# Attention and a soft mixture of experts on one core: undivided combine weights, row sums on TensorE, dispatched sums in q's PSUM bank

## The chip, the cores and the metric

The kernel runs on one core of one Trainium2 chip. The metric is the device time of one execution in microseconds (us), less is better. A run is named by the median of its executions.

## What is computed

Sliding-window causal attention over 8 batches, 8 heads, 576 positions and head size 64, and behind it a soft mixture of experts over the 4608 tokens that the attention gives (512 numbers each).

```python
scores = (1.0 / np.sqrt(D)) * np.matmul(q, k.transpose(0, 1, 3, 2))
rel = pos[:, None] - pos[None, :]
scores = np.where((rel >= 0) & (rel < 64), scores, -1000000000.0)
attn = softmax(scores, axis=-1)                    # with 1e-09 in the divisor
x = (attn @ v).transpose(0, 2, 1, 3).reshape(4608, 512)

logits = x @ phi                                   # phi: 512 x 32 slots
d = exp(logits - logits.max(0)); d /= d.sum(0)     # dispatch, over the tokens
slot_input = (d.T @ x).reshape(8, 4, 512)          # 8 experts, 4 slots each
slot_out[e] = np.maximum(slot_input[e] @ w1[e], 0) @ w2[e]   # hidden size 1024
c = exp(logits - logits.max(1)); c /= c.sum(1)     # combine, over the slots
out = c @ slot_out                                 # 4608 x 512, float32
```

## The kernel before

All inputs are float32 in memory and are cast to float16 by the loads themselves, which GpSimd issues into one queue (software_dynamic in the profile). The order of all work is written out by hand: the program order of each engine is the order of the calls, and an engine that waits holds everything behind it.

**The loop over pairs.** `n` counts 32 pairs of heads; four pairs make a batch. Step `n` works on several pairs at different stages: it transposes k of pair n+1 and q of pair n (L293), copies them to SBUF (L304, L309), takes the row maxima of pair n-1 from PSUM bank pair `a_m` (matmuls L319 and L322, VectorE's reduction L326, the ninth block in L332, L333 and L336), turns the maxima into a bias row (`st_shift`, L339 and L340), computes scores and their exponentials for pair n-2 (L345, L348, L354), multiplies pair n-4 with v (`st_av`, L378) and divides (L387, L388). `x_b` is the attention's output of a batch. v of odd rows is shifted by GpSimd (L166, L168) as soon as its load has landed, and PE's L378 needs the shifted copy. `loads(n)` issues the loads of q, k, v and of the expert weights, at fixed steps; a pool has four buffers for q and four for k, and the last expert's weights go through the same buffers (`load_last1` for w1 in four pieces `w1h`, `load_half` for w2 in two column halves of two loads each, `w2h`).

**The mixture's share of the loop.** Per batch `b`, spread over later steps: logits in columns 320 to 511 of bank `a_q` (L416), their running maximum, the exponentials `d` for the dispatch, their transposition, `fr_slots` (L503, L506: five matmuls that form the dispatched sums in `a_m`) and `fr_acc` (L514: VectorE adds them into `acc`), `fr_stat` (L446). Columns 448 to 511 of `a_q` hold -1e30, set once at L199, for the rows that have no token there. The combine weights: `fr_turn`, `cb_max` (L457), `cb_sub` on GpSimd (L462), `cb_exp` on ScalarE (L467), `cb_sum` on VectorE (L473, L474: sum over the slots and its reciprocal), `cb_mul` on GpSimd (L481), `cb_turn` (L486: transposition into `ct_all`).

**After the loop** the same steps follow in an order of their own for the last pairs, with `fill` matmuls (L624) in between, and then the experts: `first` (L793) multiplies the slots with w1 of four experts at a time, `turn_hidden` transposes, `second` (L814) multiplies with w2, for the left and the right half of the 512 columns (`ops[0]`, `ops[1]`, copied to `osb` at L879 and L883). `spread` (L646, L649) brings the combine weights of a batch into `ct4[k]`, two batches per `k`, through the tile `rp`, of which there is one. `give` (L872, L874, L876) forms the output: matmuls of 128 tokens with `osb` into one of four PSUM tiles `cp`, a copy of each tile to SBUF by ScalarE and VectorE in turn, and a store that SyncE issues. For k=0 the left half of the columns goes out first, in three stores, while the right half is still computed, then the right half in two; for k=1 to 3 nine stores of three rows of 512 columns each.

Of the kernel before, what the change touches and what calls it, by code (L numbers as in the profile page):

```python
# [18 lines left out]
def kernel(  # L19
# [178 lines left out]
    zero_q(0)  # L198
    nc.vector.memset(a_q[:, 448:512], -1.0e30)  # L199

# [229 lines left out]
    def fr_turn(b):  # L430
        lgT = pw.tile([128, 6, 32], FP32, name="lgT", tag="lgT") if b < B - 1 else lhf[0]
        nc.vector.transpose(lgT[:, :, :].rearrange("p i s -> p (i s)"), lgq[b][:, :])
        lgs[b] = lgT
# [11 lines left out]
    def fr_stat(b):  # L445
# [3 lines left out]

    lhf = [lh[:, 3 * i:3 * i + 3, :].rearrange("p i x -> p (i x)").bitcast(FP32).rearrange("p (i s) -> p i s", s=32)  # L450
           for i in range(2)]

# [12 lines left out]
    def cb_exp(b):  # L465
        ec = pw.tile([128, 6, 32], FP32, name="ec", tag="lgec") if b < B - 1 else lhf[1]
        nc.scalar.activation(ec[:, :, :], lgs.pop(b)[:, :, :], AF.Exp)  # L467
        cbs[b] = ec

    def cb_sum(b):  # L470
        pool = pw if b < B - 1 else pmo
        rs = pool.tile([128, 6], FP32, name="rs", tag="rs")
        nc.vector.reduce_sum(rs[:, :], cbs[b][:, :, :], axis=AXX)  # L473
        nc.vector.reciprocal(rs[:, :], rs[:, :])  # L474
        cbs[b] = cbs[b], rs

    def cb_mul(b, eng):
        ec, rs = cbs[b]
        cc = pw.tile([128, 6, 32], FP16, name="cc", tag="cc") if b < B - 1 else \
            lh[:, 6:8, :].rearrange("p i x -> p (i x)")[:, 0:192].rearrange("p (i s) -> p i s", s=32)  # L480
        eng.tensor_tensor(out=cc[:, :, :], in0=ec[:, :, :],  # L481
                          in1=rs[:, :].unsqueeze(2).broadcast_to([128, 6, 32]), op=ALU.mult)
        cbs[b] = cc
# [57 lines left out]
    for n in range(-1, NP - 1):  # L541
        loads(n)
        lb, eb, sb, cb = [of(n, lag) for lag in range(8, 12)]
        if of(n, 12) is not None:
            cb_sub(of(n, 12), nc.gpsimd)
        if of(n, 17) is not None:
            cb_mul(of(n, 17), nc.gpsimd)
        def maxima():
# [6 lines left out]

        if live(n - 3):
            st_score8(n - 3)
        early = n < 4
        if early and live(n - 1):
            maxima()  # L560
        if early and live(n):
            st_transpose(n, "qs", a_qh)
            st_copy_q(n)
# [43 lines left out]
        if sb is not None:  # L607
            fr_acc(sb, fr_slots(sb))
            fr_stat(sb)
# [6 lines left out]
        if of(n, 16) is not None:  # L616
            cb_sum(of(n, 16))
        if of(n, 19) is not None:
            cb_turn(of(n, 19))

# [20 lines left out]
    def spread(b, copy, rp=None):  # L641
        if rp is None:
            rp = psr.tile([128, 1024], FP32, name="rp", tag="rp")
        for t in range(5):
            w = 128 if t < 4 else 64
            nc.tensor.matmul(rp[:, 128 * t:128 * t + w], ss4[:, min(t, 3), :],  # L646
                             ct_all[:, b, 128 * (t // 4):128 * (t // 4) + w], start=True, stop=True,
                             skip_group_check=True)
        copy(out=ct4[b // 2][:, :, 64 * (b % 2):64 * (b % 2) + 64],  # L649
             in_=rp[:, 0:S].rearrange("p (x e) -> p e x", e=NE))  # L650

    b, p = B - 1, NP - 1
# [169 lines left out]
    cb_sub(b - 2, nc.gpsimd)  # L822
    cb_turn(b - 4)
    cb_sum(b - 3)
    cb_mul(b - 3, nc.gpsimd)
    first(0, 1)
# [8 lines left out]
    second(0, 0)  # L835
    cb_sum(b - 2)
    turn_hidden(1)
    spread(2, act)
    cb_mul(b - 2, nc.gpsimd)
    cb_turn(b - 3)  # L840
    cb_exp(b - 1)
    second(1, 0)
    spread(3, act)
    cb_sum(b - 1)
    cb_mul(b - 1, nc.gpsimd)
    cb_exp(b)
# [15 lines left out]
    def give(k, e0, ne, c0, nc_):  # L862
# [5 lines left out]
        for i0 in range(0, ne, n1):  # L868
            n_ = min(n1, ne - i0)
            cp = pst.tile([128, n1, nc_], FP32, name="cp", tag="cp")  # L870
            for i in range(n_):
                nc.tensor.matmul(cp[:, i, :], ct4[k][:, e0 + i0 + i, :], osb[:, c0:c0 + nc_],  # L872
                                 start=True, stop=True, skip_group_check=True)
            (act, dve)[turn % 2](out=ob[:, i0:i0 + n_, :], in_=cp[:, 0:n_, :])  # L874
            turn += 1
# [43 lines left out]
```

## Time and profile before

| | us |
|---|---|
| median of 3 runs (lowest, highest) | 194.87 (194.28, 195.09) |
| the profiled execution, its own time | 193.74 |
| its span in the trace | 192.0 |
| busy: TensorE, VectorE, ScalarE, GpSimd | 160.3, 140.1, 142.6, 102.2 |

The profiled execution's time is 1.74 us more than its span, for what lies around the program, and 1.13 us less than the median. In the rows of the profile PE is TensorE's matmuls, PEld its weight loads, DVE VectorE, ACT ScalarE, POOL GpSimd, SP SyncE. L12 is a line of the kernel. A row of the timeline has the start and the duration in us, then engine, line, operation, output and inputs by the program's names, shapes and a count; in square brackets stands how long the engine was idle just before, and what ended that. In a table by stretches the numbers behind a stretch are its length, the busy time of PE, PEld, DVE, ACT and POOL with the instructions in brackets, the share of its full clock that TensorE was granted (PEclk), the mean busy share of the 16 DMA engines, and what these moved in GB/s.

### The profile page before, as it was taken

To read this page: it belongs to the slowest core of one execution; us is meant where nothing else is said; L and a number is where in the kernel's file an instruction comes from. 1 tells how busy PE (TensorE), PEld (TensorE's weight loads), DVE (VectorE), ACT (ScalarE), POOL (GpSimd) and SP (SyncE) were. 2 spreads that over 40 slices of the span, in tenths; PEclk is the share of its full clock that TensorE was granted. 3 is DMA by queue.
4 is the path that set the end of the run, shared out by engine and by line. 5 is a ranking of instruction groups with operands and counts; after the bars stand their busy time and mean duration, and the time that the engine had idled before them with its cause. 6 is when DMAs were issued, how large, how long until landed. Compare 5 with 4: busy or idle time off the path is not lost.

```text
span 192.0 us, 6965 instructions
## 1 busy us (share of the span) xinstructions
PE 160.3 (84%) x2998; PEld 120.6 (63%) x2998; DVE 140.1 (73%) x347; ACT 142.6 (74%) x263; POOL 102.2 (53%) x131
## 2 busy tenths in 40 slices
PE   5696999989999998999999999989999899789000
PEld 1465878867777686777767786776785358542000
DVE  6683686887879779878978887897887746499100
ACT  5567979989799898989889888989578444588100
POOL 7968917455596555892993928665844133000000
PEclk9879999999999999999999999999999999999955
DMA  5999999999999999999999999999999999599995
GB/s 69 166 174 185 229 173 223 179 218 184 185 223 179 215 187 185 214 187 186 214 187 199 205 185 203 193 203 201 214 211 215 213 200 134 155 342 414 415 417 236
DMA packets 59774, 40.88 MB, mean 213 GB/s; under 512 B 38752, under 2 KB 55392, under 8 KB 58848
## 3 DMA queue, kind: packets, MB, share of 16 engines
q0 software_dynamic: 55536, 30.94, 115.6%
q1 hardware_dynamic: 4208, 9.50, 13.0%
q8 instruction: 23, 0.38, 0.7%
q14 instruction: 7, 0.06, 0.1%
HBM read 61.93 MB, written 9.44 MB: 372 GB/s over the span
## 4 chain that ended last, share of the span: by engine, by line
PE 47%; DVE 29%; ACT 7%; DMA 5%; issue 4%; POOL 0%; ACTq 0%; DVEq 0%; SPq 0%; POOLq 0%
DVE m L326 13%; PE a_m L319 6%; PE a_m L322 5%; PE a_v L378 5%; DVE x_b L388 4%; PE a_q L293 4%; DVE rt L340 3%; DMA out_dram<-w 3%; PE op L814 3%; PE a_k L293 3%; ACT qb L309 3%; DVE kT L301 2%; DMA qs<-in_q_dram 2%; PE a_s L345 2%; PE a_s L348 2%
## 5 line engine op out<-in xcount | busy, mean ns | idle before, releaser
L309 ACT ACTIVATE qb<-a_q 64x576 f16<-64x576 f16 x64 | 41.2, 644 | 7.0 <-PE a_q L293 6.2
L326 DVE TENSOR_REDUCE m<-a_m 128x8 f16<-128x1024 f32 x32 | 39.2, 1224 | 2.2 <-PE a_m L322 1.3
L354 ACT ACTIVATE pt<-a_s 128x1024 f16<-128x1024 f32 x32 | 32.8, 1024 | 6.5 <-PE a_s L348 5.1
L166 POOL COPY v<-v 64x1152 f16<-64x1152 f16 x16 | 18.2, 1140 | 28.1 <-DMA v<-in_v_dram 27.9
L388 DVE TENSOR_TENSOR x_b<-a_v,rc 128x640 f16<-128x640 f32 x31 | 25.5, 824 | 1.1
L322 PEld LDWEIGHTS <-qb 128*128 128x128 f16 x256 | 17.2, 99 | 8.5 <-ACT qb L309 1.4
L348 PEld LDWEIGHTS <-lh 128*128 128x128 f16 x288 | 18.8, 98 | 3.0 <-issue 2.6
L322 PE MATMUL a_m<-kT,qb 128*128 128x128 f16 x256 | 20.0, 222 | 0.1
L159 POOL DMA_DIRECT2D v<-in_v_dram x16 | 19.8, 1240 | 0.0
L406 ACT COPY xt<-a_k 128x576 f16<-128x576 f16 x28 | 17.9, 640 | 2.6 <-PE a_k L402 1.6
L319 PE MATMUL a_m<-wm,ident_h 128*128 128x512 f16 x64 | 19.7, 391 | 0.0
L345 PEld LDWEIGHTS <-kT 128*128 128x128 f16 x288 | 18.6, 98 | 1.6 <-issue 1.4
L345 PE MATMUL a_s<-qb,kT 128*128 128x128 f16 x256 | 19.5, 219 | 0.0
L348 PE MATMUL a_s<-rt,lh 128*128 128x128 f16 x256 | 19.5, 219 | 0.0
L168 POOL COPY v<-v 64x1088 f16<-64x1088 f16 (+1 forms) x16 | 17.9, 1117 | 0.8
L79 POOL DMA_DIRECT2D ks<-in_k_dram x17 | 11.7, 691 | 11.5 <-PE a_k L293 4.0
L340 DVE CAST rt<-a_v 9x128 f16<-9x128 f32 x30 | 8.7, 289 | 12.3 <-PE a_v L339 12.1
L378 PE MATMUL a_v<-v,pt 128*64 128x65 f16 x558 | 15.5, 196 | 2.3 <-DVE m L336 1.0
L304 ACT ACTIVATE kT<-a_k 128x576 f16<-128x576 f16 x25 | 16.3, 654 | 0.8 <-PE a_k L293 0.7
L293 PE MATMUL a_q<-ident_h,qs 96*64 96x96 f16 x384 | 15.4, 208 | 1.4 <-DMA qs<-in_q_dram 1.4
L378 PEld LDWEIGHTS <-pt 128*64 128x64 f16 x576 | 13.4, 110 | 4.5 <-DVE m L336 1.8
L293 PE MATMUL a_k<-ident_h,ks 96*64 96x96 f16 x384 | 14.6, 214 | 0.4 <-DMA ks<-in_k_dram 0.4
(174 smaller groups left out, 324.5 us busy)
## 6 DMA issues: line engine op xcount, KB each, us to landing
w<-in_moe_w_dram POOLq DMA_DIRECT2D x14, 1024.0 KB, 16.5
out_dram<-w SPq DMA_DIRECT2D x9, 768.0 KB, 8.8
qs<-in_q_dram POOLq DMA_DIRECT2D x16, 288.0 KB, 12.6
v<-in_v_dram POOLq DMA_DIRECT2D x16, 288.0 KB, 12.8
ks<-in_k_dram POOLq DMA_DIRECT2D x15, 288.0 KB, 15.4
out_dram<-w SPq DMA_DIRECT2D x2, 640.0 KB, 4.2
w1h<-in_moe_w_dram POOLq DMA_DIRECT2D x4, 256.0 KB, 16.1
w2h<-in_moe_w_dram POOLq DMA_DIRECT2D x4, 256.0 KB, 17.3
```

What stands on the lines that cost most here:

```text
L159: nc.gpsimd.dma_start(out=v1s[b % 2][:, c, 0:Dh], in_=v[b].rearrange("h s d -> (h s) d").rearrange("(c p) d -> p c d", p=128)[:, c, :])
L166: nc.gpsimd.tensor_copy(out=v2[64:128, c0:c1, 0:Dh], in_=v1[0:64, c0:c1, 0:Dh])
L293: nc.tensor.transpose(tq[64 * hf:64 * hf + 64, RP * r:RP * r + RP], src[0:RP, h + hf, Dh * r:Dh * r + Dh], ident_h[0:RP, 0:RP])
L309: nc.scalar.activation(qbs[p % NQ][h, :, hf, :], turned(a_qh)[h], AF.Copy, scale=QKS)
L319: nc.tensor.matmul(a_m[:, j, :], ident_h[:, :], wm[:, j:j + 4, :].rearrange("p c x -> p (c x)"), start=True, stop=False, skip_group_check= ...
L322: nc.tensor.matmul(a_m[:, i // 4, 128 * (i % 4):128 * (i % 4) + 128], qblock(p, i), kwindow(p, i), start=False, stop=True, skip_group_chec ...
L326: nc.vector.reduce_max(ms[p % 2][:, 64:72].rearrange("p (l c) -> p l c", l=2), a_m[:, :, :].rearrange("p l (c x) -> p l c x", x=128), axis ...
L345: nc.tensor.matmul(at(i), kwindow(p, i), qblock(p, i), start=(i % 4 == 0), stop=False, skip_group_check=True)
L348: nc.tensor.matmul(at(i), lh[:, i, :], rt[:, :], start=False, stop=True, skip_group_check=True)
L354: nc.scalar.activation(st_pt(p)[:, 0:8, :].rearrange("p i x -> p (i x)"), a_s[:, :, :], AF.Exp, scale=XS)
L378: nc.tensor.matmul(a_v[r0:r0 + 64, hf, 65 * (i // 2):65 * (i // 2) + 65], pt[:, i, 64 * hf:64 * hf + 64], rhs, start=True, stop=True, skip ...
L388: nc.vector.tensor_tensor(out=xbs[b][:, :, 128 * hp:128 * hp + 128].rearrange("p c (l d) -> p l c d", l=2), in0=avv[:, :, :, 0:64], in1=rc ...
```

## The change

Four things change. (1) In the loop `fr_slots` writes the dispatched sums into bank `a_q` in place of `a_m`; they cover all 512 columns, so VectorE sets columns 448 to 511 to -1e30 again behind `fr_acc`. (2) `cb_sum` and `cb_mul` go: `cb_exp` writes float16, and `cb_turn` transposes the undivided exponentials, three steps earlier. (3) A new function `sums(k)` multiplies the undivided weights in `ct4[k]` with a column of ones on TensorE, nine matmuls of one column into `rp`, and VectorE takes the reciprocals; the copies of the output multiply by them, one instruction per 128 tokens, since each has its own column of reciprocals. The stores for k=0, whose tiles held two groups of 256 columns, so take two copies per tile. (4) In the first four steps the ninth block's scores (`st_score8`) stand behind the maxima and not ahead of them.

```diff
-    nc.vector.memset(a_q[:, 448:512], -1.0e30)
+
+    def no_token():
+        nc.vector.memset(a_q[:, 448:512], -1.0e30)
+
+    no_token()
...
     def cb_exp(b):
-        ec = pw.tile([128, 6, 32], FP32, name="ec", tag="lgec") if b < B - 1 else lhf[1]
+        ec = pw.tile([128, 6, 32], FP16, name="ec", tag="ec") if b < B - 1 else \
+            lh[:, 6:8, :].rearrange("p i x -> p (i x)")[:, 0:192].rearrange("p (i s) -> p i s", s=32)
         nc.scalar.activation(ec[:, :, :], lgs.pop(b)[:, :, :], AF.Exp)
         cbs[b] = ec
-
-    def cb_sum(b):
...
-        nc.vector.reduce_sum(rs[:, :], cbs[b][:, :, :], axis=AXX)
-        nc.vector.reciprocal(rs[:, :], rs[:, :])
-    def cb_mul(b, eng):
...
-        eng.tensor_tensor(out=cc[:, :, :], in0=ec[:, :, :],
-                          in1=rs[:, :].unsqueeze(2).broadcast_to([128, 6, 32]), op=ALU.mult)
...
-        if of(n, 17) is not None:
-            cb_mul(of(n, 17), nc.gpsimd)
...
-        if live(n - 3):
+        early = n < 4
+        if live(n - 3) and not early:
             st_score8(n - 3)
-        early = n < 4
         if early and live(n - 1):
             maxima()
+        if live(n - 3) and early:
+            st_score8(n - 3)
...
         if sb is not None:
-            fr_acc(sb, fr_slots(sb))
+            fr_acc(sb, fr_slots(sb, a_q[:, :]))
+            no_token()
             fr_stat(sb)
...
         if of(n, 16) is not None:
-            cb_sum(of(n, 16))
-        if of(n, 19) is not None:
-            cb_turn(of(n, 19))
+            cb_turn(of(n, 16))
...
+    one = pmo.tile([128, 1], FP16, name="one")
+    nc.vector.memset(one, 0.0)
+    nc.vector.memset(one[0:32, :], 1.0)
+    rcs = pmo.tile([128, B // 2, NE], FP32, name="rcs")
+
+    def sums(k):
+        rp = psr.tile([128, 1024], FP32, name="rp", tag="rp")
+        for e in range(NE):
+            nc.tensor.matmul(rp[:, e:e + 1], ct4[k][:, e, :], one[:, :], start=True, stop=True, skip_group_check=True)
+        nc.vector.reciprocal(rcs[:, k, :], rp[:, 0:NE])
...
     first(1, 1)
     second(0, 0)
-    cb_sum(b - 2)
+    sums(0)
     turn_hidden(1)
     spread(2, act)
-    cb_mul(b - 2, nc.gpsimd)
-    cb_turn(b - 3)
     cb_exp(b - 1)
+    cb_turn(b - 2)
     second(1, 0)
     spread(3, act)
-    cb_sum(b - 1)
-    cb_mul(b - 1, nc.gpsimd)
     cb_exp(b)
-    cb_turn(b - 2)
+    cb_turn(b - 1)
+    cb_turn(b)
     for d in range(2):
         second(d, 1, range(3))
-    cb_sum(b)
-    cb_mul(b, nc.gpsimd)
-    cb_turn(b - 1)
-    cb_turn(b)
+    sums(1)
...
-            (act, dve)[turn % 2](out=ob[:, i0:i0 + n_, :], in_=cp[:, 0:n_, :])
+            for i in range(n_):
+                rc = rcs[:, k, e0 + i0 + i:e0 + i0 + i + 1]
+                if turn % 2:
+                    nc.vector.tensor_scalar(out=ob[:, i0 + i, :], in0=cp[:, i, :], scalar1=rc, scalar2=None, op0=ALU.mult)
+                else:
+                    nc.scalar.activation(ob[:, i0 + i, :], cp[:, i, :], AF.Copy, scale=rc)
             turn += 1
...
             give(k, e0, 3, 0, D)
-            if k < 3 and e0 < 6:
-                spread(2 * k + 2 + e0 // 3, (act, dve)[turn % 2])
+            if k < 3:
+                if e0 < 6:
+                    spread(2 * k + 2 + e0 // 3, (act, dve)[turn % 2])
+                else:
+                    sums(k + 1)
```

More of the change, by code (lines that the diff above doesn't have):

```diff
@@ L430, in fr_turn @@
     def fr_turn(b):
-        lgT = pw.tile([128, 6, 32], FP32, name="lgT", tag="lgT") if b < B - 1 else lhf[0]
+        lgT = pw.tile([128, 6, 32], FP32, name="lgT", tag="lgT") if b < B - 1 else lhf
         nc.vector.transpose(lgT[:, :, :].rearrange("p i s -> p (i s)"), lgq[b][:, :])
@@ L447, in fr_stat @@
                                 op0=ALU.mult, op1=ALU.add)
-    lhf = [lh[:, 3 * i:3 * i + 3, :].rearrange("p i x -> p (i x)").bitcast(FP32).rearrange("p (i s) -> p i s", s=32)
-           for i in range(2)]
+    lhf = lh[:, 0:3, :].rearrange("p i x -> p (i x)").bitcast(FP32).rearrange("p (i s) -> p i s", s=32)
     def cb_max(b):
@@ L822 @@
     cb_sub(b - 2, nc.gpsimd)
-    cb_turn(b - 4)
-    cb_sum(b - 3)
-    cb_mul(b - 3, nc.gpsimd)
+    cb_turn(b - 3)
     first(0, 1)
```

7 lines of the change are left out of this document (removed).

## The prediction

> **What bounds the kernel now.** I read the page first, its slices and its list of DMA issues, then the output phase by half microseconds.
>
> ```profile
> DMA  5999999999999999999999999999999999599995
> v<-in_v_dram POOLq DMA_DIRECT2D x16, 288.0 KB, 12.8
> 164.50:165.00 0.50, 0.46 (x5) 0.26 (x3) 0.45 (x1) 0.50 (x2) 0.00 (x0) 1.00 0.02 2
> 165.50:166.00 0.50, 0.50 (x7) 0.43 (x5) 0.34 (x1) 0.23 (x1) 0.00 (x0) 1.00 0.16 53
> 166.00:166.50 0.50, 0.27 (x3) 0.10 (x1) 0.00 (x0) 0.20 (x1) 0.00 (x0) 1.00 1.04 340
> 189.50:190.00 0.50, 0.00 (x0) 0.00 (x0) 0.00 (x0) 0.00 (x0) 0.00 (x0) 0.50 0.78 320
> ```
>
> The DMA engines are busy in every slice but the first, one near the end and the last. Half of the loads of v land 12.8 us or more after their issue, while the engines are busy: a load finds others queued ahead of it, and the queue does not run dry. The input is therefore one stream in the order of issue, whose landing times the engines' work does not move. One hole follows, around 164.5 (share 0.02). From 166.0 to 190 the output fills the DMA engines again. The end is thus: the last input lands, the experts' last matmuls and the first copies follow, the first store is issued, and about 24 us of stores follow.
>
> Next I asked each late load when it lands (start of its issue plus time to landing), and the timeline when it is used.
>
> ```profile
> L131 POOL DMA_DIRECT2D w1h<-in_moe_w_dram x2: 548/550/551, 137.3 to 137.9; - x2
> DMA to landing us min/median/max: 16.1/16.5/16.8
> L141 POOL DMA_DIRECT2D w2h<-in_moe_w_dram x1: 742/742/742, 145.1 to 145.1; - x1
> DMA to landing us min/median/max: 17.2/17.2/17.2
> L141 POOL DMA_DIRECT2D w2h<-in_moe_w_dram x1: 740/740/740, 147.6 to 147.6; - x1
> DMA to landing us min/median/max: 17.4/17.4/17.4
> 153.32 2.12 PE L793 MATMUL ha<-w,sit 128*32 128x512 f16 x35
> 155.72 0.38 PE L793 MATMUL ha<-w1h,sit 128*32 128x512 f16 x1
> 162.53 0.93 PE L814 MATMUL op<-w2h,hT 128*32 128x256 f16 x7
> 163.50 0.37 ACT L879 CAST qb<-op 128x256 f16<-128x256 f32 x1 [1.91 <-PE op L814]
> 164.38 1.35 ACT L874 COPY w<-cp 128x512 f32<-128x512 f32 x3 [0.51 <-PE cp L872]
> 164.99 15.94 SPq L876 DMA_DIRECT2D out_dram<-w  x14
> 165.22 1.05 PE L814 MATMUL op<-w2h,hT 128*32 128x256 f16 x8
> 166.30 0.37 ACT L883 CAST qb<-op 128x256 f16<-128x256 f32 x1 [0.57 <-PE op L814]
> ```
>
> The last two pieces of w1 land at about 153.5 and 154.7 (137.3 + 16.1, 137.9 + 16.8); the last is used at 155.72, 1.0 us later. The left half of w2 is complete at 145.1 + 17.2 = 162.3; its second load is used by the last four of the seven matmuls from 162.53, at 162.86, 0.6 us later. The right half is complete at 165.0 and its second load used by the fifth of the eight from 165.22, at about 165.7. So work ahead of the experts that ends earlier can bring the first store forward by at most 0.6 us.
>
> **The loop: the dispatched sums leave `a_m`.** One such step:
>
> ```profile
> 80.25 1.23 DVE L326 TENSOR_REDUCE m<-a_m 128x8 f16<-128x1024 f32 x1
> 81.53 0.40 PE L503 MATMUL a_m<-x_b,dT 128*32 128x512 f16 x4 [0.46 <-DVE m L326]
> 82.35 0.75 DVE L514 SCALAR_TENSOR_TENSOR acc<-acc,al,a_m 128x512 f32<-128x512 f32 x1 [0.68 <-PE a_m L506]
> 83.01 0.27 DVE L446 TENSOR_SCALAR stat<-stat,al,s 128x1 f32<-128x1 f32 x1
> 83.20 0.21 DVE L387 RECIPROCAL rc<-a_v 128x10 f32<-128x10 f32 x1
> L199 DVE MEMSET a_q<- 128x64 f32 x1 | 0.1, 112 | 0.1
> ```
>
> TensorE waits 0.46 for VectorE's maxima to leave `a_m`, then VectorE waits 0.68 for the sums. In `a_q`, which was copied out earlier in the step, the five matmuls run 0.5 earlier, beside the maxima, and VectorE's addition follows the maxima at once: 0.6 earlier, less 0.1 for the new memset of 0.11. The memset waits for the addition on VectorE itself; behind it stand L446 and the division, so its price is in the 0.1. TensorE's transpositions of the next q into `a_q` must now wait for the addition (and perhaps the memset), which end near 82.6; they stand behind the multiplication with v, which takes TensorE to about that time, so this wait costs 0 to 0.1 and holds only the next maxima. Gain 0.5 a batch, six times, the first at 48 us.
>
> **The loop: no sum, no division of the weights.** The transposition of `cb_turn` is only moved.
>
> ```profile
> L473 DVE TENSOR_REDUCE rs<-ec 128x6 f32<-128x192 f32 x7 | 2.4, 340 | 0.5 <-ACT ec L467 0.5
> L474 DVE RECIPROCAL rs<-rs 128x6 f32<-128x6 f32 x8 | 1.5, 192 | 0.3
> 15.04 0.22 PE L345 MATMUL a_k<-qb,kT 128*128 128x128 f16 x1 [0.82 <-ACT kT L304]
> 51.24 1.09 POOL L168 COPY v<-v 64x1088 f16<-64x1088 f16 x1
> 52.42 0.36 PEld L378 LDWEIGHTS <-pt 128*64 128x64 f16 x17 [0.31 <-DVE m L336]
> ```
>
> VectorE loses 0.53 a batch, four times inside the loop, at most 2.1; part of it lies under TensorE's multiplication with v, which the division awaits anyway, so I take 0.3 each, 1.2. GpSimd loses a multiplication a batch; it waits for landings in most steps, so nothing there. The scores moved behind the maxima in the first steps save at most the 0.82 at 15 us. But all that is saved before 52 us is lost again: the shifted v is ready at 51.24 + 1.09 = 52.33, just behind a landing, and used at 52.42. So 0.82 and the first 0.5 count nothing, and the loop saves 5 x 0.5 + 1.2 = 3.7, at most; I take 3.5, with 2 to 4 as bounds. The experts' first matmul comes at 149.8 in place of 153.32.
>
> **The stall that follows.** From 149.8 the first 40 matmuls of L793 take 2.2 us, four at a time, then TensorE stands from about 152.1 to 153.5 and again from 153.8 to 154.7 for the last two pieces of w1. Of the 3.5 us only 1.0 is left behind it, and that not by any engine but by the stream of loads.
>
> ```profile
> 5.00:7.00 2.00, 0.62 (x22) 0.43 (x16) 1.75 (x5) 0.65 (x1) 2.00 (x3) 1.00 1.26 180
> 8.00:12.00 4.00, 3.92 (x42) 2.38 (x41) 2.36 (x7) 2.63 (x5) 3.48 (x5) 0.57 1.62 150
> 12.00:14.00 2.00, 2.00 (x50) 1.83 (x48) 1.45 (x4) 1.37 (x3) 1.02 (x2) 1.00 1.44 188
> ```
>
> TensorE busy for 0.62 of two microseconds was followed by four in which it was granted 0.57 of its clock, though busy all the time. The stall, about 2.2 us idle of three, is as thin. Whether it lowers the clock is a rival below; the sum goes without. The Trainium skill, "TensorE: Matmul & The Clock Gate", Part 1, lets the clock fall only after an idle window of about 3.4 us, and warns of gaps longer than that: by this rule stalls of 1.4 and 0.9 us with matmuls between cost nothing, and the time stays at 195.2. The rows differ from it, since matmuls ran in that stretch too.
>
> **The experts and the first store.** `sums(0)` and `sums(1)` stand in TensorE's order ahead of the left half's last matmuls.
>
> ```profile
> 158.84 0.32 PEld L646 LDWEIGHTS <-v 128*128 128x128 f16 x5
> L874 ACT COPY w<-cp 128x256 f32<-128x256 f32 x1 | 0.4, 390 | 0.0
> L874 DVE COPY w<-cp 128x256 f32<-128x256 f32 x1 | 0.4, 414 | 0.0
> L799 ACT ACTIVATE hs<-ha,emask 128x512 f16<-128x512 f32 x2 | 1.4, 689 | 2.4 <-PE ha L793 2.4
> L809 ACT COPY hT<-th 128x512 f16<-128x512 f16 x2 | 1.2, 582 | 1.3 <-PE th L808 1.3
> ```
>
> Five weight loads of 128 columns start 0.056 apart (0.32 less one of 0.1, by four), so nine take 0.5, and the two calls 1.0; bounds 0.4 (one lies in waits that TensorE has there) and 1.5. `rp` has one buffer, so `spread(2)` also waits for the reciprocal of `sums(0)` (0.19 by L474), which the transpositions between them hide. With 1.0 earlier at the start and 1.0 more work, the left half is ready at 163.5 as before, and 162.3 is no limit any more.
>
> ScalarE's copy of 256 columns is 0.39, and a scale from a column adds 689 - 582 = 107 ns, so 0.5; two, overlapping a little, take 0.95 in place of about 0.6 for the one of 512. VectorE's two take about 0.9. The first store leaves 0.35 later, at 165.3 (bounds 0.2 and 0.6). The right half follows: its matmuls wait for the first `cp` tile, 0.35 later, and ScalarE's five small copies last to 164.38 + 2 x 0.95 + 0.45 = 166.7, so L883 is at 166.7. Is the output's queue then ever empty? Before, bytes moved 0.9 us after the first issue. Now 256 + 256 + 640 KB at 340 GB/s last from 166.2 to about 169.7; the fourth store needs L883 and about 2 us, 168.7, plus 0.9: just in time. Later stores hold 768 KB, 1.9 us of transfer, and need three copies, about 1.1 us on two engines; the 27 scaled copies, `sums(2)` and `sums(3)` lie under the stores.
>
> **The sum.** Own time 193.74; experts -1.0 + 1.0; first copies +0.35; stores the same length: 194.1. On the median, 194.87 + 0.35 = 195.2 us. Its own range, with the bounds above (experts -0.6 to +0.5, copies 0.2 to 0.6) is 194.5 to 196.0.
>
> **Rivals.** *Half clock behind the stall.* For: the rows from 5 to 14 us. Against: with a loop that saves under 3 us the first stall is under 1 us. The four microseconds at 0.57 lost 4 x 0.43 = 1.7 us of full clock; behind the stall the matmuls are all on the path, so the same costs 1.7 there. It decides from about 2 us of idleness in three. 195.2 + 1.7 = 196.9, slower. Chance 0.17.
>
> *The saving does not reach the experts.* If the wait of the q transpositions for `a_q` takes the place of the one removed, or another load is late, less than 0.3 us is left at 153: then `sums` and copies stand uncovered, +1.35, 196.2. For: v was 0.09 us ahead at 52 us. Against: the waits at 80 us are plain and nothing else ended last there. Chance 0.12.
>
> *The path was in the engines, not in the loads.* The median is 1.13 us above the profiled execution; if the others lose that in the loop, the saved 3.5 absorbs it (195.2 - 1.13 = 194.1), and if the loads moved up as well, the whole would show: 194.87 - 3.5 + 1.35 = 192.7. I take 193.3, between them. For: 142 us of busy ScalarE. Against: the unbroken DMA row. Chance 0.13.
>
> **Chances.** Forecast 0.58, rivals 0.17, 0.12 and 0.13. Half a per cent, 0.97 us, is about what a measurement of this kernel can tell from no change. The forecast lies within it, the first two rivals above, the third below: faster 0.13, same 0.58, slower 0.29. The range takes in the forecast's own, the two slower cases, and the third rival in part: 193.9 to 196.9.
>
> **What would show it.** Right: the shifts of v and the late loads land when they did, within 0.5 us; VectorE's idle 0.68 before L514 is gone; L793 starts near 150 and waits for `w1h`; the first store leaves within 0.5 us of 165.3. Wrong: the last `w2h` lands a microsecond or more earlier; PEclk below 1.00 between 154 and 166; DMA share under 0.9 between 167 and 189; L793 not before 152.5.

## The result, and the profile after

| | before | after |
|---|---|---|
| median, run side by side (lowest to highest) | 194.98 (194.28 to 197.51) | 192.48 (192.22 to 192.86) |
| the profiled execution, its own time | 193.74 | 192.86 |
| its span | 192.0 | 191.1 |
| busy: TensorE, VectorE, ScalarE, GpSimd | 160.3, 140.1, 142.6, 102.2 | 161.9, 139.2, 144.6, 97.9 |

The ratio is 0.9885 (95% interval 0.985 to 0.992): the change makes the kernel 2.5 us faster by the medians and 2.2 by the ratio, where 195.2 and a range from 193.9 were forecast. Ratios are of undisturbed executions alone, medians of all, so the two differ a little in places. The two profiled executions are only 0.9 us apart; the rest of the difference is between executions that left no profile, and that is the first thing to explain.

The page of after answers to the first rows of before:

```profile
DMA  4999999999999999999999999999999999499996
v<-in_v_dram POOLq DMA_DIRECT2D x16, 288.0 KB, 12.7
```

The DMA engines are as full as before, with the same hole before the stores. The late loads of after, by the issue of two pieces of w1 and of the last load of either half of w2:

```profile
L131 POOL DMA_DIRECT2D w1h<-in_moe_w_dram x2: 543/548/553, 136.6 to 137.1; - x2
DMA to landing us min/median/max: 16.6/17.0/17.3
...
L141 POOL DMA_DIRECT2D w2h<-in_moe_w_dram x1: 747/747/747, 144.9 to 144.9; - x1
DMA to landing us min/median/max: 17.2/17.2/17.2
...
L141 POOL DMA_DIRECT2D w2h<-in_moe_w_dram x1: 740/740/740, 147.3 to 147.3; - x1
DMA to landing us min/median/max: 17.4/17.4/17.4
```

The last w1h lands at 137.15 + 17.3 = 154.45, the left half of w2 at 162.06, the right at 164.7: 0.2 before the times of the kernel before. The timeline of the experts and the first store in after:

```profile
152.07 2.12 PE L793 MATMUL ha<-w,sit 128*32 128x512 f16 x35
154.49 0.38 PE L793 MATMUL ha<-w1h,sit 128*32 128x512 f16 x1
157.20 0.38 PE L649 MATMUL rp<-one,v 128*128 128x1 f16 x9
161.47 0.38 PE L649 MATMUL rp<-one,v 128*128 128x1 f16 x9
161.78 1.05 PE L814 MATMUL op<-w2h,hT 128*32 128x256 f16 x8
162.87 0.37 ACT L877 CAST qb<-op 128x256 f16<-128x256 f32 x1 [2.28 <-PE op L814]
164.62 1.47 SPq L874 DMA_DIRECT2D out_dram<-w  x3
```

L793 starts 1.25 earlier, not 3.5, so TensorE does not stand before w1h: its last piece is used at 154.49, 0.04 after it landed. The loop itself saved more. From the first maxima to the last it took 127.31 us in after and 130.16 before, 2.85 less; but in this execution the first q landed at 7.89 in place of 6.59, and the first maxima came 1.60 later (11.16, 9.56). The transposition of the first q, before and then after:

```profile
6.63 0.45 PE L293 MATMUL a_q<-ident_h,qs 96*64 96x96 f16 x12 [1.38 <-DMA qs<-in_q_dram]
```

```profile
7.94 0.45 PE L297 MATMUL a_q<-ident_h,qs 96*64 96x96 f16 x12 [2.62 <-DMA qs<-in_q_dram]
```

Behind the last w1h the sums cost 0.3 us each (nine matmuls at 161.47, the next work at 161.78), and the first store leaves 0.37 earlier than before. It is followed by 26.5 us to the end of the span, before by 27.0.

One batch's first step, in after, and the next maxima of both kernels:

```profile
80.44 1.22 DVE L330 TENSOR_REDUCE m<-a_m 128x8 f16<-128x1024 f32 x1
82.01 0.75 DVE L503 SCALAR_TENSOR_TENSOR acc<-acc,al,a_q 128x512 f32<-128x512 f32 x1
82.84 0.11 DVE L201 MEMSET a_q<- 128x64 f32 x1
83.01 0.45 PE L297 MATMUL a_q<-ident_h,qs 96*64 96x96 f16 x12 [0.20 <-DVE a_q L201]
84.96 1.23 DVE L330 TENSOR_REDUCE m<-a_m 128x8 f16<-128x1024 f32 x1
```

```profile
85.01 1.22 DVE L326 TENSOR_REDUCE m<-a_m 128x8 f16<-128x1024 f32 x1
89.33 1.22 DVE L326 TENSOR_REDUCE m<-a_m 128x8 f16<-128x1024 f32 x1
93.71 1.23 DVE L326 TENSOR_REDUCE m<-a_m 128x8 f16<-128x1024 f32 x1
```

VectorE's idle 0.68 before the addition is gone but for 0.14; yet the step is 84.96 - 80.44 = 4.52 long where it was 85.01 - 80.25 = 4.76: 0.24 less. Most of the other half of the expected 0.5 stands in the fourth row: TensorE waits 0.20 for the new memset before it may write q into the bank. The two steps behind it, without sum and division of the weights, are 4.20 and 4.21 long in after (84.96, 89.16, 93.37), before 4.32 and 4.38.

### The profile page after: what moved, and what is told of

Read it like the earlier page. It is cut to its first block, busy times and chain, and to the rows that moved or that the text cites. A ratio compares the mean times of both kernels' runs of the same rounds, so it can differ in the third digit from the quotient of the medians.

```text
span 191.1 us, 7035 instructions
## 1 busy us (share of the span) xinstructions
PE 161.9 (85%) x3034; PEld 121.7 (64%) x3034; DVE 139.2 (73%) x347; ACT 144.6 (76%) x267; POOL 97.9 (51%) x123
## 4 chain that ended last, share of the span: by engine, by line
PE 50%; DVE 24%; ACT 8%; DMA 6%; issue 4%; POOL 1%; ACTq 0%; DVEq 0%; POOLq 0%
DVE m L330 9%; PE a_m L323 6%; PE a_m L326 6%; PE a_q L297 5%; PE a_v L382 4%; PE a_s L349 4%; PE a_s L352 4%; DVE x_b L392 3%; DMA out_dram<-w 3%; PE op L814 3%; DMA ks<-in_k_dram 3%; DVE acc L503 3%; ACT qb L313 2%; DVE rt L344 2%; PE a_k L406 2%
## 5 line engine op out<-in xcount | busy, mean ns | idle before, releaser
L326 PEld LDWEIGHTS <-qb 128*128 128x128 f16 x256 | 17.3, 99 | 8.5 <-ACT qb L313 1.3
L297 PEld LDWEIGHTS <-qs 96*64 96x64 f16 x384 | 12.2, 111 | 5.6 <-DMA qs<-in_q_dram 2.8
## 6 DMA issues: line engine op xcount, KB each, us to landing
w2h<-in_moe_w_dram POOLq DMA_DIRECT2D x4, 256.0 KB, 17.3
```

The costliest lines, as they stand in the source:

```text
L297: nc.tensor.transpose(tq[64 * hf:64 * hf + 64, RP * r:RP * r + RP], src[0:RP, h + hf, Dh * r:Dh * r + Dh], ident_h[0:RP, 0:RP])
L326: nc.tensor.matmul(a_m[:, i // 4, 128 * (i % 4):128 * (i % 4) + 128], qblock(p, i), kwindow(p, i), start=False, stop=True, skip_group_chec ...
```

## The experiments

**Before once more, and the parts alone.** The kernel before, unchanged, beside three kernels that have one part each:

```diff
 # p1_slots
-            fr_acc(sb, fr_slots(sb))
+            fr_acc(sb, fr_slots(sb, a_q[:, :]))
+            no_token()
 # p4_order
-        if live(n - 3):
+        if live(n - 3) and not early:
             st_score8(n - 3)
         if early and live(n - 1):
             maxima()
+        if live(n - 3) and early:
+            st_score8(n - 3)
 # p23_undivided: the diff of the change without these two
```

> The kernel before, unchanged, for the spread of its executions and for another profile of it. Theory A (the start differs between executions): in the profile of before the first q landed at 6.59, in the profile after at 7.89, and the median of before lies 1.1 us over its profiled execution. By A this profile has its first q between 6.6 and 7.9, the experts' first matmul L793 later by the same difference (153.3 to 154.6), and its own time is higher by it (193.7 to 195.0); the timed runs spread over 194.3 to 195.1. Theory B (the difference lies elsewhere, in the stream of loads or in the stores): the own time does not follow the first landing; L793 stays at 153.3 within 0.3 whatever the first landing.

> Before, with the dispatched sums in q's bank and the memset behind the addition, and nothing else of the change. By the steps of the two traces: the step with the sums is 4.52 in place of 4.76 us from one maxima to the next, six times: 1.4 us earlier at L793. Theory A (in a usual execution of before no load stands close enough to take it back): faster by 1.4 us, about 193.5. Theory L (the loads set the end, as predicted): w1h lands near 154.5 and its last use is 1.0 before that, so at most 1.0 of it is left: 194.0 or more.

> Before, with only the scores moved behind the maxima in the first steps. Between the first maxima and the fourth the trace after took 11.45 us, before 12.30: 0.85 less. Theory A: it comes through to the end, 194.0 to 194.2. Theory L, as predicted: it is lost again where the shifted v of the fourth pair of loads is used at 52 us, and the time is that of before, within 0.2.

> Before, with undivided weights, sums on TensorE and scaled copies alone; the dispatched sums stay in a_m and the order of the first steps as before. By the steps: in two of a batch's four steps 0.13 and 0.18 us less, three or four times, 0.9 to 1.2 us; two sums of 0.31 us and 0.26 at the first copies are spent, 0.88. Theory A: between no change and 0.4 us faster, 194.5 to 194.9. Theory L: up to 1.0 saved at w1h and 0.88 spent, 194.8 to 195.0. As predicted in the sum (copies 0.35, sums 1.0, saving 1.2 of which 1.0 counts): 195.2. If the copies or sums cost more at the end than the trace after shows, it is slower than 195.2.

| | median | of before in the same runs | ratio (95%) |
|---|---|---|---|
| before again | 194.61 | 194.53 | 1.0015 (0.9988, 1.0042) |
| slots alone | 193.26 | 194.53 | 0.9940 (0.9910, 0.9970) |
| order alone | 194.29 | 194.53 | 0.9962 (0.9934, 0.9990) |
| undivided alone | 194.59 | 194.53 | 0.9992 (0.9962, 1.0021) |

The parts add up to the whole within their intervals: -0.6, -0.4 and -0.1% against -1.15%. The slots bring 1.2 to 1.3 us, near six steps at 0.24 (1.4). That is the time of theory A; by theory L, the prediction's, at most 1.0 could pass the wait for w1h. The undivided weights bring nothing by themselves, again within theory A: what the loop gains, the sums and copies spend. The order brings 0.2 by the medians and 0.7 by the ratio (0.2 to 1.3), so these runs do not tell whether most of its 0.85 comes through. Its profiled execution lost most of it. Its ninth maxima came 0.74 before those of before (41.61, 42.35), its thirteenth 0.18 (59.05, 59.23), for between them TensorE met the shifted v of 52 us:

```profile
52.31 0.41 PE L378 MATMUL a_v<-v,pt 128*64 128x65 f16 x15 [0.40 <-POOL v L168]
```

That the saving of the first steps is lost there is what the prediction said. It does not hold in every execution: in both profiles of after TensorE did not wait for v at this place.

The second profile of before (own time 196.19, 2.45 over the first) refutes both theories in their first form. Its first q landed at 6.25, earlier than in the first profile, and yet its start was slower, by 0.36 because the second k landed later (7.74, 7.38), and for the rest by TensorE's rate:

```profile
8.41 1.03 PE L319 MATMUL a_m<-wm,ident_h 128*128 128x512 f16 x2
9.24 1.06 PE L322 MATMUL a_m<-kT,qb 128*128 128x128 f16 x8
11.61 1.01 PE L319 MATMUL a_m<-wm,ident_h 128*128 128x512 f16 x2
12.54 1.03 PE L322 MATMUL a_m<-kT,qb 128*128 128x128 f16 x8
23.36 1.23 DVE L326 TENSOR_REDUCE m<-a_m 128x8 f16<-128x1024 f32 x1
...
165.33 0.60 PE L814 MATMUL op<-w2h,hT 128*32 128x256 f16 x4 [0.41 <-DMA w2h<-in_moe_w_dram]
```

In the first profile of before the timeline reads at these places:

```profile
7.81 0.61 PE L319 MATMUL a_m<-wm,ident_h 128*128 128x512 f16 x2
11.77 0.65 PE L322 MATMUL a_m<-kT,qb 128*128 128x128 f16 x8
21.86 1.22 DVE L326 TENSOR_REDUCE m<-a_m 128x8 f16<-128x1024 f32 x1
```

And the table by stretches from 60 to 80 us (the last two columns are the DMA share and GB/s), the first profile and then the second:

```profile
60.00:80.00 20.00, 18.74 (x404) 15.31 (x402) 16.48 (x41) 17.82 (x34) 11.87 (x15) 1.00 1.57 194
```

```profile
60.00:80.00 20.00, 18.39 (x393) 15.14 (x392) 16.97 (x41) 17.76 (x34) 10.54 (x13) 1.00 1.68 186
```

A pair of 512 columns takes 0.61 at full rate and 1.0 at half. In the second profile TensorE ran at half from 6.3 to 14.2, in the first from 8.5 to 11.9, and the fourth maxima came at 23.36 in place of 21.86: 1.5 us. Besides, its DMA engines, always busy, moved 186 GB/s where the first had 194 between 60 and 80 us, and the last w1h landed at 157.7 in place of 154.7; this time before, too, waited for w2h (0.41). The delay arose around the loads of v: ten of the sixteen landed 2.4 to 3.4 us after the load ahead of them, in the first profile none more than 2.1 (why is not known). So executions of one kernel differ in two things: how long TensorE's start is slow, and how fast the stream of loads runs.

**Are the loads the limit of after?** Theory L says that they are; theory E says that the engines set the end. Four kernels: after once more; the sums moved out of the path; less work in the loop, by leaving out the dispatched sums of the batches 1 to 5 (`a_lite`, whose output misses them); and the same with the four loads of w1h left out as well.

```diff
 # a_sums_late
     second(0, 0)
-    sums(0)
     turn_hidden(1)
...
-    sums(1)
...
     second(0, 1, (3,))
+    sums(0)
...
     second(1, 1, (3,))
+    sums(1)
 # a_lite
-            fr_acc(sb, fr_slots(sb, a_q[:, :]))
-            no_token()
+            if sb == 0:
+                fr_acc(sb, fr_slots(sb, a_q[:, :]))
+                no_token()
+            else:
+                dts.pop(sb), xbs.pop(sb)
 # a_lite_now1h: the same, and in load_last1
-        a = pin.tile([128, F], FP16, name="w1h", tag="qs")
-        nc.gpsimd.dma_start(out=a, in_=w1_dram(last)[:, len(w1_t[last]), :])
-        w1_t[last].append(a)
+        w1_t[last].append(w1_t[0][len(w1_t[last])])
```

> The kernel after, unchanged, for the size of the difference and for a second profile of it. From the parts alone (slots -1.3, order -0.2, undivided +0.1 in medians): about 1.4 us under before if they only add up in medians, 2.1 by the ratios of undisturbed runs. Theory E (the engines set the end in a usual execution): a second profile with a warmer start than the first (first maxima before 10.5 in place of 11.16) has L793 earlier by the same and is shorter by up to 1 us. Theory L (the stream of loads sets the end): L793 earlier, but the last use of w1h and w2h stays within 0.2 of their landing, and the time moves only with the landings.

> After, with both sums moved behind the last matmuls of each half, where TensorE waits some 0.45 us for ScalarE's copy of the experts' output. Theory E: two times 0.31 us leave the path to the first store, 0.6 us faster than after. Theory L: in the profile after the left half's second load of w2 landed at 162.06 and was used at 162.23, so at most 0.2 comes through; TensorE then waits for w2h ahead of the fifth matmul of the half, as in the second profile of before (0.57 us). If the reciprocals come too late for the first copies, the first store does not move at all or is later.

> After, leaving out the dispatched sums, their addition and the memset for the batches 1 to 5 in the loop (the output misses them). Five steps of 4.5 us become about 3.85: 3 us less of engine work ahead of the experts. Theory E: 3 us faster than after, about 189.5. Theory L, which is the mechanism of the prediction: L793 starts near 149, TensorE waits for w1h, whose last landing stays near 154.5, and the end is at most 0.5 earlier than that of after: 192.0 or more. If the stall behind w1h also halves the clock, as the first rival of the prediction has it, 193.5.

> The same, and the four loads of w1h left out as well (the last expert uses the first one's w1, so its output is another): 1 MB less in the stream ahead of w2h, at 210 GB/s 5 us. Theory L: with the loads 5 us earlier the engines' saving comes through: 189 to 190, 2.5 to 3 us below the kernel that leaves out the sums alone. Theory E: no difference between the two, both near 189.5.

| | median | of before in the same runs | ratio (95%) |
|---|---|---|---|
| after again | 192.18 | 194.26 | 0.9873 (0.9828, 0.9918) |
| sums late | 192.12 | 194.26 | 0.9866 (0.9822, 0.9911) |
| lite | 193.51 | 194.26 | 0.9949 (0.9906, 0.9991) |
| lite, no w1h | 189.82 | 194.26 | 0.9745 (0.9692, 0.9798) |

The last two show the mechanism: less work ahead of the experts made the kernel 1.3 us slower than after (193.5 was expected if the stall halves the clock), and the same kernel without four loads is 3.7 us faster than that. The timeline of the lite kernel:

```profile
151.31 0.40 PE L796 MATMUL ha<-w,sit 128*32 128x512 f16 x3
153.23 0.38 PE L796 MATMUL ha<-w1h,sit 128*32 128x512 f16 x1 [1.52 <-DMA w1h<-in_moe_w_dram]
154.46 0.58 PE L796 MATMUL ha<-w1h,sit 128*32 128x512 f16 x1 [0.83 <-DMA w1h<-in_moe_w_dram]
```

Its table by stretches, cut where the granted clock changes (the last three columns are the granted clock, the DMA share and GB/s):

```profile
150.69:154.10 3.41, 1.42 (x23) 0.44 (x16) 1.01 (x2) 0.31 (x1) 0.50 (x1) 1.00 1.09 215
154.10:157.51 3.41, 3.05 (x25) 1.38 (x28) 0.68 (x2) 1.43 (x3) 0.51 (x1) 0.50 1.21 201
```

It is the prediction's stall in the prediction's place, with its first rival behind it: 1.52 and 0.83 us idle, then 3.41 us with the clock at half. L793 started at 149.16, near the 149.8 of the prediction, and the last w1h still landed at 154.4. It was used at 154.46, as in after (154.49), and yet the first store left at 165.93 in place of 164.62: the 1.3 us arise behind the stall. The Trainium skill, "TensorE: Matmul & The Clock Gate", Part 1, lets the clock fall after an idle window of about 3.4 us and makes of it a rule against idle gaps of that length. Here it fell after two shorter waits with matmuls between them, so the measurement decides against that rule for gaps.

The second profile of after (own time 191.88) started faster and met the stall in its mild form:

```profile
150.93 2.12 PE L793 MATMUL ha<-w,sit 128*32 128x512 f16 x35
153.30 0.40 PE L793 MATMUL ha<-w,sit 128*32 128x512 f16 x3
153.60 0.38 PE L793 MATMUL ha<-w1h,sit 128*32 128x512 f16 x1
163.69 1.47 SPq L874 DMA_DIRECT2D out_dram<-w  x3
```

Its last two loads of w1:

```profile
L131 POOL DMA_DIRECT2D w1h<-in_moe_w_dram x2: 546/550/553, 136.1 to 136.6; - x2
DMA to landing us min/median/max: 16.3/16.6/16.9
```

The last group of four at 153.30 is held by its w1h, which landed at 153.56 and ran at 153.60. So this execution is 0.98 shorter than the first, about what its loads were earlier (0.9), though its engines were 1.14 ahead: theory L, as far as one execution tells.

Moving the sums brought nothing in the time, though in the profile the stretch from the last L793 to L877 is 5.56 us in place of 6.47 and 6.43: the fifth matmul of the left half then used its w2h 0.04 after the landing (161.67, 161.63). The same profile, with an early start, shows such a stall at another place, the shifted v of 52 us (its timeline, then its table by stretches, cut where the granted clock changes):

```profile
51.38 0.22 PE L382 MATMUL a_v<-v,pt 128*64 128x65 f16 x2 [1.33 <-POOL v L166]
52.53 0.42 PE L382 MATMUL a_v<-v,pt 128*64 128x65 f16 x15 [0.93 <-POOL v L168]
```

```profile
50.12:53.54 3.42, 1.24 (x46) 1.06 (x46) 0.80 (x4) 1.27 (x3) 3.30 (x3) 1.00 1.95 188
53.54:56.96 3.42, 3.42 (x31) 2.80 (x27) 1.62 (x3) 2.13 (x4) 3.33 (x6) 0.50 1.15 226
```

Again two waits, 1.33 and 0.93, and the clock at half behind them. The next maxima came 3.2 us later than elsewhere in the loop, and the execution still took only 192.28.

**A later start, and fewer loads, in both kernels.**

```diff
 # b_late, a_late
-            st_copy_q(n)
+            for _ in range(2 if n == 0 else 1):
+                st_copy_q(n)
 # a_now1h, b_now1h: load_last1 as in a_lite_now1h
```

> Before, with ScalarE's two copies of the first pair's q done twice: 1.3 us more ahead of the first maxima, on the engines alone; the loads are issued as before. Theory A (in before the engines set the end, and the loads stand 0.6 to 1.0 behind them): 1.3 us later less what the wait for v at 52 us takes back in an execution with an early start, so 0.8 to 1.3 slower than before. If the loads set the end of before as well: 0 to 0.4.

> After, with the same two copies done twice. Theory L (the loads set the end of after, with 0 to 0.3 to spare): the 1.3 us vanish in the wait for w1h in executions with an early start and count in part in those with a late one: 0.1 to 0.6 slower than after's 192.2. Theory E (the engines set it): 0.8 to 1.3 slower, as in before.

> After, without the four loads of w1h (the last expert uses the first one's w1). Theory L: the stream ends 5 us earlier and no longer holds the experts; the engines' own end shows, 0.3 to 1.0 below after, about 191.5; the executions then spread as those of before do. Theory E: no change from 192.2.

> Before, without the four loads of w1h. Its loads have 0.6 to 1.0 us to spare in three of four profiles and stood in the way in one (w1h at 157.69, own time 196.19). Theory A (the start makes the difference between its executions): no change of the median, within 0.2, and the long executions remain. Theory D (late loads make it): the median falls by 0.5 or more and the executions above 195.5 go.

| | median | of before in the same runs | ratio (95%) |
|---|---|---|---|
| before, late | 195.49 | 194.20 | 1.0074 (1.0046, 1.0102) |
| after, late | 193.08 | 194.20 | 0.9938 (0.9913, 0.9963) |
| after, no w1h | 191.81 | 194.20 | 0.9881 (0.9854, 0.9907) |
| before, no w1h | 193.66 | 194.20 | 0.9974 (0.9949, 0.9999) |

Before loses the whole 1.3. After loses 0.6 to 0.9 against its two medians (192.48, 192.18) and 1.0 to 1.3 by the ratios: more than theory L said, and by the ratios as much as theory E. Its profile has the fourth maxima at 23.75, the last w1h landed at 154.40 and used at 155.28: with this start the engines set the end. The copies are not the whole of that delay, for in this profile the granted clock was 0.50 from 9.2 to 16.0 us, twice as long as in the first profile of after. Without w1h after gains 0.4 in the median and nothing by the ratio; before gains 0.5, and its longest executions remain (196.2 and 197.3 among twelve), so that neither the start alone (theory A) nor late loads alone (theory D) make the difference between its executions. So in after the engines and the loads are within half a microsecond of each other, and the execution decides which comes last; in before the engines are mostly later, not always.

**A faster start, and the load order at the end.**

```diff
 # b_warm, a_warm
         if early and live(n):
+            if n == 0:
+                warm_up(4)
             st_transpose(n, "qs", a_qh)
 # a_split; a_split_late is this with the sums late
-    load_w(13)
     for d in range(2):
+        for h in range(2):
+            nc.gpsimd.dma_start(out=w2_t[NRES - 1, 0][:, 4 * h:4 * h + 4, DH * d:DH * d + DH],
+                                in_=w2_dram(NRES - 1)[:, h, :, DH * d:DH * d + DH])
         load_half(d)
 # a_left_first: a_split_late, and
-    for d in range(2):
-        second(d, 1, range(3))
+    second(0, 1, range(3))
...
+    second(1, 1, range(3))
     second(1, 1, (3,))
```

> Before, with four more warm-up matmuls (128x512, on zeros and ones) between the transpositions of the first k and of the first q, where TensorE waits for the first q. In the profiles the matmuls from 6 to 14 us ran at half rate for 3.3 us in the profile of before and for 7.7 us in its second one, and the fourth maxima came at 21.86 and 23.36. Theory A (this start is why the median of before lies above its profile): more executions start at full rate, fourth maxima near 21.5, the median falls by 0.5 to 1.0. Theory D (the rate of the loads, which landed up to 3 us later in the second profile): the median does not move by more than 0.2.

> After, with the same four matmuls. Theory L: an earlier start only lengthens the waits for v at 52 us and for w1h: no change from 192.2, within 0.2, or slower where such a wait halves TensorE's rate behind it. Theory E: 0.5 to 1.0 faster.

> After, with the second layer of the seventh expert loaded in halves by columns, its right half behind the left half of the last expert: the left half of the output then needs 0.5 MB less of the stream, 2.4 us at 210 GB/s, and the last load lands when it did. Theory L (the left half's w2h sets the first store): w2h's left half lands near 159.7 and the first store leaves 0.2 earlier at most, since the sums keep the engines at 162.2: 192.0. Theory E: the same, no change. It is the base for the next one.

> The same with both sums behind the last matmuls of each half. Theory L: moving the sums brought nothing while w2h landed at 162.06 (192.12 against 192.18); with the left half's loads out of the way the 0.6 us come through at the first store, 191.6, as far as the later stores keep the queue full. Theory E (sums of such a size never were on the path): 192.1.

> The loads in halves and the sums late as before, and the seventh expert's right half no longer ahead of the left half's last matmuls in TensorE's order: experts 4 to 6 of the right half follow the left half's copies. In the two kernels with halves TensorE stood 0.67 and 0.78 us for that right half, which landed behind the left one. Theory L: the left half's loads are all in near 159.7, the engines have it ready near 161.0 in place of 162.9, the first store leaves near 162.9 in place of 163.7 to 164.6; the right half waits for its last load (164 to 165) and its first store leaves near 167.5 as before, so that the queue runs thin in between: 191.2 to 191.9, under both kernels. Theory E: the left half is not earlier, and the right half is 0.7 later by the matmuls moved: 192.5 or more.

| | median | of before in the same runs | ratio (95%) |
|---|---|---|---|
| before, warm | 194.37 | 194.78 | 0.9961 (0.9927, 0.9996) |
| after, warm | 192.39 | 194.78 | 0.9885 (0.9857, 0.9913) |
| split | 194.13 | 194.78 | 0.9967 (0.9945, 0.9989) |
| split, sums late | 193.26 | 194.78 | 0.9927 (0.9899, 0.9956) |
| left first | 192.14 | 194.80 | 0.9893 (0.9848, 0.9939) |

The warmer start makes before 0.4 us faster (by the ratio 0.8), after not at all: what it saves there goes into the waits for v and w1h (1.19 and 0.64 us in its profile). The long executions of before remain with it (196.5, 198.7), so the start is only a part of the spread; the rate of the loads is the other that the profiles show, and their shares stay open.

The split alone, expected at 192.0, is slower than after, for a reason that neither theory had: TensorE's program has experts 4 to 6 of both halves ahead of the last expert's left half, so the right half of expert 6, now loaded later, held the left. The profile with late sums:

```profile
161.33 0.62 PE L816 MATMUL op<-w,hT 128*32 128x256 f16 x12 [0.67 <-DMA w<-in_moe_w_dram]
162.73 0.29 PE L816 MATMUL op<-w,hT 128*32 128x256 f16 x3 [0.78 <-DMA w<-in_moe_w_dram]
```

In the split kernel sums(1) stood behind the stall and sums(0) ahead of it, and moving both gave 0.9 (0.8 by the ratios, too wide to tell from the 0.3 of sums(1)): they are on the path where no load covers them. The last kernel takes that wait out of the order, and its first store leaves 1.7 to 2.7 us earlier than in the profiles of after. Yet its time is that of after, between what the two theories gave (its timeline, then its table by stretches):

```profile
161.97 5.49 SPq L873 DMA_DIRECT2D out_dram<-w  x4
164.54 0.60 PE L816 MATMUL op<-w2h,hT 128*32 128x256 f16 x4 [0.73 <-DMA w2h<-in_moe_w_dram]
```

```profile
166.50:167.00 0.50, 0.19 (x3) 0.06 (x1) 0.50 (x2) 0.50 (x3) 0.00 (x0) 1.00 0.36 125
167.00:167.50 0.50, 0.49 (x2) 0.13 (x2) 0.50 (x2) 0.50 (x3) 0.00 (x0) 1.00 0.04 12
167.50:168.00 0.50, 0.15 (x1) 0.10 (x1) 0.50 (x2) 0.50 (x2) 0.00 (x0) 1.00 0.01 2
```

The early stores are out at 166.8 and the queue is empty until 168, because the right half waits for the last load. None of these kernels beats after by more than its interval.

## Why the prediction was wrong

The mechanism exists: the lite kernel, 2.9 us ahead of after at L793, had its last w1h at 154.4 as after had, and the stall, the halved clock behind it and the loss of an early start at 52 us were all measured, but in other kernels; of the two profiles of the change itself one met no stall and one 0.3 us of it. Two steps of the prediction failed: that of the loop's saving only 1.0 us passes the wait for w1h, and that the median of after lies as far above its profile as that of before. Both took one execution of before for the kernel. Besides, four terms had the wrong size. The sum by terms, from the profile of before to the two of after:

| | forecast | after | after again |
|---|---|---|---|
| L793 starts | -3.5 | -1.25 | -2.39 |
| stall behind w1h | +2.5 | 0 | +0.3 |
| sums, to L877 | +1.0 | +0.6 | +0.55 |
| copies, to the first store | +0.35 | +0.25 | +0.25 |
| first store to the end | 0 | -0.5 | -0.6 |
| own time | +0.35 | -0.9 | -1.9 |
| own time to the median | +1.13 | -0.4 | +0.3 |

- *"On the median, 194.87 + 0.35 = 195.2 us."* Here the error is 1.5 of 2.7 us with the first profile of after (1.13 counted, -0.4 measured) and 0.8 of 3.0 with the second. The 1.13 between the profile of before and its median was added to after as if it belonged to the kernel. It was chance, as far as the other executions tell: of the seven profiles of kernels with the old order the first had the earliest fourth maxima (21.86; the others 21.96, with a start made warmer, to 23.97, with one made late), and of 35 executions of before only 4 were shorter than its 193.74. The profiles of after lie on both sides of its medians. The third rival said that the median's excess would be absorbed if it arose in the loop, and gave 193.3. The time went its way, but its reason was seen only in part: a warmer start helps before and not after, while a later one costs after nearly as much. Its chance of 0.13 was too low for the one rival that asked what a single profile could not show.
- *"Of the 3.5 us only 1.0 is left behind it."* The step took 154.68 for a fixed time, and the 1.0 us of slack in one execution for the slack of the kernel. The slots alone brought 1.2 to 1.3, and before made 1.3 us late lost all of it: in most executions of before the engines come last, not w1h. An estimate from the rows of the first two profiles and the median of before says the same. If the whole saving of the loop passes, and sums, copies and stores count as measured, 194.98 - 2.85 + 0.6 + 0.25 - 0.5 = 192.5, which is the time measured. That the first profile of after, with -1.25 up to the last w1h, stands so near to the -1.0 of the sum is luck: its start was 1.60 late. The landing moves as well. In the sixteen profiles with these loads the last w1h landed between 153.56 and 157.69; in those of after at 154.45 and 153.56. In place of 1.0 the last use of w1h came 1.2 and 2.1 earlier (155.72; 154.49 and 153.60). Ten profiles with undivided weights have it at 153.56 to 154.60, six with divided ones at 154.33 to 157.69; whether GpSimd's multiplication, which stood ahead of loads in its order, delays them was not tried. In the second profile of before it ran beside none of the late loads of v.
- *"Gain 0.5 a batch."* It was 0.24, mostly because the wait of the q transpositions for `a_q`, taken at 0 to 0.1, was 0.20. The undivided weights saved what was said (0.3 a batch) and the order 0.85 in the first steps, of which v took 0.56 in the kernel with the order alone. So the loop saved about 2.8 from the first to the last maxima (130.16 before, 127.31 after) where 3.5 was counted.
- *The sums at 1.0, from weight loads 0.056 apart.* They took 0.31 each, nine weight loads at 0.035 between matmuls of one column, where the five at 0.056 stood between matmuls of 128. Copies at 0.35: 0.25.
- *"stores the same length"*. From the first store to the end of the span it was 27.0 in before and 26.5 and 26.4 in after. Of these 0.5 us, 0.2 lie in the stores (the last one lands 25.7 us after the first is issued, in after 25.5) and 0.3 behind them, where the span of before goes on for 1.28 us and that of after for 0.98. The 0.3 is not a matter of the copies, since before without w1h, which has the old ones, also ends 0.98 after its last store. What it comes from is open.

Of the signs that the text named as right, the loads landed within 0.5 us in the first profile, and the idle 0.68 is gone; the first store (164.62) missed its half microsecond, and L793 neither started near 150 nor waited (in the second profile it started at 150.93 and its last group waited 0.3). Of those named as wrong, only one came, and only in the second profile: the last w2h landed 1.1 earlier.

## What to carry to other kernels

Before a term is added to a sum, ask whether it belongs to the kernel or to the execution: the distance of one profiled execution from the median is the second, and a kernel with slack in another place will not repeat it. Where two limits stand within a microsecond of each other, forecast the later of two that vary, and write the landing of a load as a range from several loads or runs, not as a time. A change that takes engine work away in front of a saturated load stream can make a kernel slower, if the stall that it opens lowers the clock.

## What the runs showed of the hardware

- Two short waits are enough to halve TensorE's clock: 1.52 and 0.83 us in one place, 1.33 and 0.93 in another; behind them the granted clock was 0.50 for 3.41 us. Waits of 0.40 and of some 0.3 us (order alone, after again) had no such effect, nor had 0.67 and 0.78 (split, sums late) or 0.26 and 0.93 (after, warm). How busy TensorE was in all tells them apart. In the 3.41 us ahead of a fall it was busy for 1.42 (lite), 1.24 (sums late) and 1.64 us (first profile of before, from 5.05 to 8.47). In split with sums late and in after, warm, no stretch of this length around the waits had less than 1.9. Where between 1.64 and 1.9 the limit lies was not tried.
- The start's slow phase is not always in the clock records. In the second profile of before eight matmuls of 128 columns took 1.06 and 1.03 us at 9.24 and 12.54, where they take 0.61 later, and the rows from 8 to 14 us gave a granted clock of 1.00. The time of the matmuls is the surer sign. The Trainium skill, "TensorE: Matmul & The Clock Gate", Part 1, has the array begin at half its clock and gives about 3.4 us of sustained work for the warming. The second profile does not agree: TensorE was busy without a break from 8 to 14 us and still at half its rate. The 3.4 us at half in the first profile are no test of it, since matmuls at full rate came ahead of them (the twelve at 6.63 took 0.45, at half rate 0.69).
- The rate of a saturated stream of loads is not the same in each execution: 186 against 194 GB/s over 20 us with DMA engines that never rested, 3 us by the last load.
